# First expert product: 128 channels through the whole array, the last 64 for two chunks at a time in its two halves of rows

## Chip, cores and metric

One core of a Trainium2 chip. The metric is device time in microseconds (us). Medians are of four to seven runs. Block times, clock figures and profile lines are those of each kernel's one profiled run. Ratios are computed as the mean time of one kernel's runs over the mean of the other's from the same rounds, so they are not quite the ratios of the medians quoted beside them.

## The reference

A causal convolution over the sequence (7 taps, softmax weights a head) feeds a mixture of experts with 28,672 tokens, 192 channels (D), 8 experts and a hidden width of 1024 (F). A token goes to the expert with the largest logit, or, where its local gate is at least one half, to the one that the token before it went to. Its output is the softmax probability of that expert times two products:

```python
h = np.maximum(x[b, s] @ w1[e], 0.0)     # 192 -> 1024
out[b, s] = p[e] * (h @ w2[e])           # 1024 -> 192
```

All data are fp32.

## The kernel before

Three stages: convolve and route, place every token in a slot (all 256 slots of a block belong to one expert), then 119 expert blocks. Only the last stage changes much. Three block-long pieces of work go through PE (TensorE): the first product, four transposes for the next block, the second product. In short:

```python
DG = D + 1              # a token's row: its D values, then its gate
xp = pool(name="xp", bufs=4)        # gathered rows; wp, the weights, has 3 buffers

def load(i):            # weights of block i; its 256 rows by two indirect DMAs
    ...
    for k in range(2):
        nc.gpsimd.indirect_dma_start(out=xg[:, k, :], in_=rows[:, :], ...)   # L393

def turn(i, xg):        # rows -> channels on partitions, two halves of 96
    for d in range(2):
        for k in range(2):
            nc.tensor.transpose(xps[:, d, k*P:(k+1)*P], xg[:, k, d*DH:(d+1)*DH], identity=ident)
    nc.vector.tensor_copy(xT, xps)

def hidden(w1b, xT):    # first product, four PSUM banks of two chunks each
    for m in range(0, FK, 2):
        for u in range(2):
            for d in range(2):      # 96 + 96 channels
                nc.tensor.matmul(hps[:, u, :], lhsT=w1b[:, d, (m+u)*P:(m+u+1)*P],
                                 rhs=xT[:, d, :], start=(d == 0), stop=(d == 1))
        # eviction with relu: banks 0 and 2 on ScalarE (L419), 1 and 3 on VectorE (L417)

def output(i, w2b, xg, hT):
    ...                 # second product, 16 matmuls of 192 columns
    # scaling by the gate: first half on ScalarE (L434), second on VectorE (L432),
    # then two indirect DMAs scatter the rows

for i in range(NB):
    ...                 # load(i + 2)
    hT = hidden(w1b, xT)
    xT = turn(i + 1, ...)
    output(i, w2b, xg, hT)
```

The order in which each engine's instructions stand in the program is not the order of this text. A scheduler decides it from the dependencies and its own notion of time. It moves, for instance, the gather of a later block ahead as soon as one of the four `xg` buffers is free.

## Time and profile before

| | before |
|---|---|
| time, median | 2082.5 us |
| span of the profiled run | 2076.4 us |
| one expert block, from one scaling on ScalarE to the next | 12.55 us |
| first product, of that (32 records x 0.216) | 6.91 us |
| granted clock in the expert stage | full, no exception |

And a trap, in the page's list of DMAs (the last number is the median time from issue to landing):

```profile
xg<-rows,slot_tok POOLq DMA_INDIRECT x238, 9.1
```

These 9.1 us come from a handful of gathers at the start, behind the first weight loads. In steady blocks the trace's semaphore updates show the second gather landing 2.55 us after its issue.

### The profile page before, as it was taken

The page shows a single profiled execution, that of the slowest core. Times are in us where ns is not written, and L with a number is a line of the kernel's source. Part 1 is how long each engine was busy: PE and PEld are TensorE (multiplying, and loading weights), DVE is VectorE, ACT ScalarE, POOL GpSimd, SP SyncE. Part 2 cuts the span into 40 slices and gives each one's busy share as a digit, 9 for nine tenths or more (in the row PEclk, how much of TensorE's full clock was granted, in tenths as well). Part 3 has the DMA queues.
Part 4 walks back from the last instruction along what each step waited for, and adds up shares of the span by engine and source line. Part 5 has one row for each costly group of instructions (what it writes and reads, how often), then busy time and mean ns, then how long its engine had stood idle before and what let it go on. Part 6 is the DMA issues. An engine that isn't in the chain of part 4 may idle for free. (4 is left out here: it accounts for less than half of the span.)

```text
span 2076.4 us, 25966 instructions
## 1 busy us (share of the span) xinstructions
PE 1953.5 (94%) x10208; PEld 1679.0 (81%) x10208; DVE 594.2 (29%) x1648; ACT 257.6 (12%) x487; POOL 494.7 (24%) x521
## 2 busy tenths in 40 slices
PE   2989889589699999999999999999999999999998
PEld 1868667511199999999999999999999999999997
DVE  5333333599711111111111112111111211111111
ACT  0211112000011111111111111111111111111111
POOL 3000000000123333333333333333333333333331
PEclk9989879555599999999999999999999999999999
DMA  3362441300265555555555555555555555555551
GB/s 107 104 160 88 130 121 40 98 9 1 61 175 152 160 162 156 154 159 157 153 155 163 157 153 156 163 155 153 162 161 154 153 160 158 152 158 163 156 154 34
DMA packets 111547, 278.60 MB, mean 134 GB/s; under 512 B 12639, under 2 KB 77367, under 8 KB 100002
## 3 DMA queue, kind: packets, MB, share of 16 engines
q1 hardware_dynamic: 59536, 209.24, 34.3%
q0 software_dynamic: 22848, 45.58, 7.5%
q10 hardware_dynamic: 29042, 22.14, 4.4%
q8 instruction: 80, 1.31, 0.3%
q14 instruction: 41, 0.34, 0.0%
HBM read 232.74 MB, written 45.53 MB: 134 GB/s over the span
## 5 line engine op out<-in xcount | busy, mean ns | idle before, releaser
L414 PE MATMUL hps<-xT,w1b 96*128 96x256 f32 x3808 | 843.2, 379 | 0.0
L414 PEld LDWEIGHTS hps<-xT,w1b 96*128 96x128 f32 x3808 | 721.2, 190 | 93.3
L426 PE MATMUL yps<-w2b,hT 128*128 128x192 f32 x3808 | 638.5, 326 | 0.0
L426 PEld LDWEIGHTS yps<-w2b,hT 128*128 128x128 f32 x3808 | 616.1, 190 | 0.1
L437 POOL DMA_INDIRECT out_dram<-o_sb,slot_tok x238 | 240.6, 1011 | 963.4 <-ACT o_sb L434 859.1
L417 DVE TENSOR_SCALAR hT<-hps 128x512 f32<-128x512 f32 x238 | 164.5, 691 | 638.3 <-PE hps L414 638.3
L393 POOL DMA_INDIRECT xg<-rows,slot_tok x238 | 232.9, 979 | 230.2 <-DVE slot_tok L366 154.5
L419 ACT ACTIVATE hT<-hps 128x512 f32<-128x512 f32 x238 | 142.1, 597 | 675.8 <-PE hps L414 673.0
L432 DVE TENSOR_SCALAR o_sb<-yps,xg 128x192 f32<-128x192 f32 x119 | 49.7, 418 | 572.7 <-ACT o_sb L434 572.7
L434 ACT ACTIVATE o_sb<-yps,xg 128x192 f32<-128x192 f32 x119 | 50.0, 420 | 804.9 <-PE yps L426 784.5
L358 PE MATMUL sps<-at_hi,at_lo 128*128 128x476 bf16 x224 | 124.4, 555 | 24.5 <-DVE at_lo L352 13.0
L186 PEld LDWEIGHTS lps<-wg,yT 96*128 96x128 f32 x896 | 126.7, 215 | 16.5 <-ACT yT L183 8.0
L165 PE MATMUL cps<-x_sb,band 128*128 128x336 f32 x256 | 100.8, 478 | 31.2 <-DVE band L79 27.1
L186 PE MATMUL lps<-wg,yT 96*128 96x9 f32 x896 | 123.3, 265 | 3.8 <-DVE yT L181 3.4
L358 PEld LDWEIGHTS <-at_lo 128*128 128x128 bf16 x224 | 23.4, 105 | 124.7 <-DVE at_lo L352 124.7
L167 PE MATMUL cps<-x_sb,pband 128*128 128x336 f32 x256 | 98.2, 467 | 10.2 <-DVE pband L79 10.2
L165 PEld LDWEIGHTS cps<-x_sb,band 128*128 128x128 f32 x256 | 48.4, 201 | 52.6 <-DVE band L79 27.3
L402 PE MATMUL xps<-ident,xg 128*96 128x128 f32 x476 | 73.3, 275 | 13.6 <-DMA xg<-rows,slot_tok 13.6
L405 DVE COPY xT<-xps 96x512 f32<-96x512 f32 x119 | 80.5, 676 | 13.4 <-PE xps L402 13.4
L402 PEld LDWEIGHTS xps<-ident,xg 128*96 128x96 f32 x476 | 56.6, 127 | 29.3 <-issue 11.8
L167 PEld LDWEIGHTS cps<-x_sb,pband 128*128 128x128 f32 x256 | 49.4, 200 | 33.0 <-DVE pband L79 11.4
L177 PE MATMUL tps<-ident,y_sb 128*96 128x128 f32 x448 | 75.4, 295 | 0.0
(114 smaller groups left out, 532.4 us busy)
## 6 DMA issues: line engine op xcount, KB each, us to landing
w1b<-in_w_dram SPq DMA_DIRECT2D x119, 768.0 KB, 5.2
w2b<-in_w_dram SPq DMA_DIRECT2D x119, 768.0 KB
rows<-y_sb ACTq DMA_DIRECT2D x16, 1351.0 KB, 7.7
x_sb<-in_x_dram SPq DMA_DIRECT2D x16, 1344.0 KB, 6.5
xg<-rows,slot_tok POOLq DMA_INDIRECT x238, 9.1
out_dram<-o_sb,slot_tok POOLq DMA_INDIRECT x238, 2.4
w<-in_weight_dram SPq DMA_DIRECT2D x1, 28.0 KB
wg<-in_wgl_dram ACTq DMA_DIRECT2D x1, 6.8 KB
```

The costliest lines, as they stand in the source:

```text
L165: nc.tensor.matmul(cps, lhsT=band[:, h, :], rhs=x_sb[:, 1 + s:1 + s + CB, hc], start=True, stop=False)
L167: nc.tensor.matmul(cps, lhsT=pband[:, h, :], rhs=x_sb[:, s:s + CB, hc], start=False, stop=True)
L186: nc.tensor.matmul(lps[:, j + u, :], lhsT=yT[:, u, k, :], rhs=wg[:, k, :], start=(k == 0), stop=(k == 1))
L358: nc.tensor.matmul(sps, lhsT=at_lo, rhs=at_hi, start=(t == 0), stop=(t == T - 1))
L393: nc.gpsimd.indirect_dma_start(out=xg[:, k, :], out_offset=None, in_=rows[:, :], in_offset=bass.IndirectOffsetOnAxis(ap=slot_tok[:, n:n + ...
L402: nc.tensor.transpose(xps[:, d, k * P:(k + 1) * P], xg[:, k, d * DH:(d + 1) * DH], identity=ident)
L405: nc.vector.tensor_copy(xT, xps)
L414: nc.tensor.matmul(hps[:, u, :], lhsT=w1b[:, d, (m + u) * P:(m + u + 1) * P], rhs=xT[:, d, :], start=(d == 0), stop=(d == 1))
L417: nc.vector.tensor_scalar(hT[:, m:m + MH, :], hps, 0.0, None, Alu.max)
L419: nc.scalar.activation(hT[:, m:m + MH, :], hps, Act.Relu)
L426: nc.tensor.matmul(yps[:, k, :], lhsT=hT[:, m, k * P:(k + 1) * P], rhs=w2b[:, m, :], start=(m == 0), stop=(m == FK - 1))
L437: nc.gpsimd.indirect_dma_start(out=out, out_offset=bass.IndirectOffsetOnAxis(ap=slot_tok[:, n:n + 1], axis=0), in_=o_sb[:, k, :], in_offse ...
```

## The change

D is 192, so two passes of 96 rows leave a quarter of the array's rows idle. The change contracts 128 channels with the whole array (8 products) and the last 64 in one half of its rows each (8 products, alternating between the halves so that two can run at once). The halves need the 64 channels on partitions 0 to 63 and again on 64 to 127. So ScalarE copies them beside themselves in `xg` before the transposes. The core of the diff (gate moved to column 0 and weight layout cut):

```diff
-        xg = xp.tile([P, KT, DG], F32, name="xg")
+        xg = xp.tile([P, KT, DG + DR], F32, name="xg")          # DR = 64
...
     def turn(i, xg):
-        xps = xps_p.tile([DH, 2, BT], F32, name="xps")
+        nc.scalar.copy(xg[:, :, DG:], xg[:, :, 1 + P:DG])        # L400
+        xps = xps_p.tile([P, 2, BT], F32, name="xps")
...
     def hidden(w1b, xT):
+        hps = [hps_p.tile([P, 2, BT], F32, name="hps") for q in range(FK // 2)]
+        for s in range(FK):                                      # L415: 128 rows
+            nc.tensor.matmul(hps[s // 2][:, s % 2, :], lhsT=w1b[:, s * P:(s + 1) * P],
+                             rhs=xT[:, 0, :], start=(s % 2 == 0), stop=False, ...)
+        for half in range(2):
+            for j in range(2):
+                for row in range(2):                             # L424: 64 rows
+                    rows_ = slice(row * DR, (row + 1) * DR)
+                    c = F + (half * 2 + j) * P
+                    nc.tensor.matmul(hps[half * 2 + row][:, j, :], lhsT=w1b[rows_, c:c + P],
+                                     rhs=xT[rows_, 1, :], start=False, stop=True, ...)
+            # evictions: bank 2*half on ScalarE (L432), bank 2*half + 1 on VectorE (L430)
```

More of the change, by code (lines that the diff above doesn't have):

```diff
@@ L27 @@
 DH = D // 2
+DR = D - P
 FK = F // P
@@ L33 @@
 NS = NB * KT
-DG = D + 1
+DG = 1 + D
 SHIFT_P = P.bit_length() - 1
@@ L163, in conv @@
                 hc = slice(h * GS, (h + 1) * GS)
+                yc = slice(1 + h * GS, 1 + (h + 1) * GS)
                 cps = cps_p.tile([P, CB, GS], F32, name="cps")
@@ L169, in conv @@
                 if h % 2:
-                    nc.vector.tensor_copy(y_sb[:, s:s + CB, hc], cps)
+                    nc.vector.tensor_copy(y_sb[:, s:s + CB, yc], cps)
                 else:
-                    nc.scalar.copy(y_sb[:, s:s + CB, hc], cps)
+                    nc.scalar.copy(y_sb[:, s:s + CB, yc], cps)
         for j in range(0, NT, 2):
@@ L176, in conv @@
                 for k in range(2):
-                    nc.tensor.transpose(tps[:, u, k, :], y_sb[:, j + u, k * DH:(k + 1) * DH],
+                    nc.tensor.transpose(tps[:, u, k, :], y_sb[:, j + u, 1 + k * DH:1 + (k + 1) * DH],
                                         identity=ident)
@@ L250, in route @@
         nc.vector.tensor_reduce(pr, ex, axis=AX.X, op=Alu.add)
-        nc.vector.tensor_tensor(y_sb[:, :, D], pr, rs, op=Alu.mult)
+        nc.vector.tensor_tensor(y_sb[:, :, 0], pr, rs, op=Alu.mult)
         for s in range(0, NT, CB):
@@ L378, in experts @@
     yps_p = ctx.enter_context(tc.tile_pool(name="yps_p", bufs=2, space=PSUM))
-    MH = 512 // BT
     def load(i):
@@ L383, in load @@
                            skip_runtime_bounds_check_because="a count of at most 7")
-        w1b = wp.tile([DH, 2, F], F32, name="w1b")
-        nc.sync.dma_start(out=w1b.rearrange("p k f -> p (k f)"),
-                          in_=w1[bass.ds(e, 1)].rearrange("o p x -> (o p) x"))
+        w1b = wp.tile([P, F + F // 2], F32, name="w1b")
+        nc.sync.dma_start(out=w1b, in_=w1[bass.ds(e, 1)].rearrange("o p x -> (o p) x"))
         w2b = wp.tile([P, FK, D], F32, name="w2b")
@@ L393, in load @@
             nc.gpsimd.indirect_dma_start(
-                out=xg[:, k, :], out_offset=None, in_=rows[:, :],
+                out=xg[:, k, :DG], out_offset=None, in_=rows[:, :],
                 in_offset=bass.IndirectOffsetOnAxis(ap=slot_tok[:, n:n + 1], axis=0))
@@ L402, in turn @@
                 nc.tensor.transpose(xps[:, d, k * P:(k + 1) * P],
-                                    xg[:, k, d * DH:(d + 1) * DH], identity=ident)
-        xT = tp.tile([DH, 2, BT], F32, name="xT")
+                                    xg[:, k, 1 + d * P:1 + (d + 1) * P], identity=ident)
+        xT = tp.tile([P, 2, BT], F32, name="xT")
         nc.vector.tensor_copy(xT, xps)
@@ L409, in hidden @@
         hT = hp.tile([P, FK, BT], F32, name="hT")
-        for m in range(0, FK, MH):
-            hps = hps_p.tile([P, MH, BT], F32, name="hps")
-            for u in range(MH):
-                for d in range(2):
-                    nc.tensor.matmul(hps[:, u, :], lhsT=w1b[:, d, (m + u) * P:(m + u + 1) * P],
-                                     rhs=xT[:, d, :], start=(d == 0), stop=(d == 1))
-            if (m // MH) % 2:
-                nc.vector.tensor_scalar(hT[:, m:m + MH, :], hps, 0.0, None, Alu.max)
-            else:
-                nc.scalar.activation(hT[:, m:m + MH, :], hps, Act.Relu)
+        hps = [hps_p.tile([P, 2, BT], F32, name="hps") for q in range(FK // 2)]
+        for s in range(FK):
+            nc.tensor.matmul(hps[s // 2][:, s % 2, :], lhsT=w1b[:, s * P:(s + 1) * P],
+                             rhs=xT[:, 0, :], start=(s % 2 == 0), stop=False,
+                             skip_group_check=True)
+        for half in range(2):
[4 more added lines that the diff above has]
+                    nc.tensor.matmul(hps[half * 2 + row][:, j, :], lhsT=w1b[rows_, c:c + P],
+                                     rhs=xT[rows_, 1, :], start=False, stop=True,
+                                     skip_group_check=True)
+            for row in range(2):
+                q = half * 2 + row
+                if row:
+                    nc.vector.tensor_scalar(hT[:, 2 * q:2 * q + 2, :], hps[q], 0.0, None, Alu.max)
+                else:
+                    nc.scalar.activation(hT[:, 2 * q:2 * q + 2, :], hps[q], Act.Relu)
         return hT
@@ L429, in output @@
         for k in range(KT):
-            gate = xg[:, k, D:D + 1]
+            gate = xg[:, k, 0:1]
             if k % 2:
@@ L451, in experts, with _w1_layout @@
         output(i, w2b, xg, hT)
+def _w1_layout(np, w1):
+    rest = w1[:, P:, :].reshape(E, DR, 2, 2, 2, P)
+    rest = rest.transpose(0, 3, 1, 2, 4, 5).reshape(E, P, F // 2)
+    return np.concatenate([w1[:, :P, :], rest], 2)
 def kernel(**inputs):
@@ L466 @@
         .reshape(2, DH, E + 1).transpose(1, 0, 2).reshape(DH, 2 * (E + 1)),
-        "w1": i["moe_w1"].reshape(E, 2, DH, F).transpose(0, 2, 1, 3).reshape(E, DH, 2 * F),
+        "w1": _w1_layout(_np, i["moe_w1"]),
         "w2": i["moe_w2"].reshape(E, FK, P, D).transpose(0, 2, 1, 3).reshape(E, P, FK * D),
```

## The prediction

> **What bounds the kernel now.** I read the page first: busy shares, then the strip of 40 slices.
>
> ```profile
> PE 1953.5 (94%) x10208; PEld 1679.0 (81%) x10208; DVE 594.2 (29%) x1648; ACT 257.6 (12%) x487; POOL 494.7 (24%) x521
> ...
> PE   2989889589699999999999999999999999999998
> ...
> PEclk9989879555599999999999999999999999999999
> ...
> L414 PE MATMUL hps<-xT,w1b 96*128 96x256 f32 x3808 | 843.2, 379 | 0.0
> ...
> L426 PE MATMUL yps<-w2b,hT 128*128 128x192 f32 x3808 | 638.5, 326 | 0.0
> ```
>
> From slice 12 on (about 575 us, to 2070) the expert blocks run: PE at nine tenths in every slice, full clock, no idle time before either product. The first product (L414), which the change touches, is the dearest group, 843.2 us. 3808 records are 119 blocks x 32: 16 products a block, each two records because the data are fp32. The mean of 379 ns is latency; start to start in the trace's records two of them are 0.216 us apart, so 32 take 6.91 us.
>
> Then I read the timeline of one block, all engines. Columns: start, length, engine, line, operation, in brackets the idle time before it.
>
> ```profile
> 1000.22 7.07 PE L414 MATMUL hps<-xT,w1b 96*128 96x256 f32 x32
> ...
> 1000.42 0.42 ACT L434 ACTIVATE o_sb<-yps,xg 128x192 f32<-128x192 f32 x1 [6.77 <-PE yps L426]
> 1000.87 0.42 DVE L432 TENSOR_SCALAR o_sb<-yps,xg 128x192 f32<-128x192 f32 x1 [4.81 <-ACT o_sb L434]
> 1001.11 1.01 POOL L437 DMA_INDIRECT out_dram<-o_sb,slot_tok  x1 [7.25 <-ACT o_sb L434]
> 1002.19 0.60 ACT L419 ACTIVATE hT<-hps 128x512 f32<-128x512 f32 x1 [1.36 <-PE hps L414]
> 1002.42 0.99 POOL L393 DMA_INDIRECT xg<-rows,slot_tok  x1 [0.30 <-issue]
> 1003.72 0.97 POOL L393 DMA_INDIRECT xg<-rows,slot_tok  x1 [0.30 <-issue]
> ...
> 1007.12 0.60 PE L402 MATMUL xps<-ident,xg 128*96 128x128 f32 x4
> ...
> 1007.56 5.37 PE L426 MATMUL yps<-w2b,hT 128*128 128x192 f32 x32
> ...
> 1012.76 1.03 PE L414 MATMUL hps<-xT,w1b 96*128 96x256 f32 x4
> ...
> 1012.97 0.42 ACT L434 ACTIVATE o_sb<-yps,xg 128x192 f32<-128x192 f32 x1 [6.77 <-PE yps L426]
> ```
>
> PE runs first product, four transposes, second product with no gap; from one scaling by ScalarE (L434) to the next is 12.55 us (over 111 blocks: 12.549 to 12.552). So the matmul stream alone sets the period. ScalarE waits most of it. What matters later: right after block i is scaled (1000.42, 1000.87), GpSimd issues a scatter and then the two gathers of a **later** block, into the buffer that block i has just left (four buffers of xg).
>
> **What the Trainium skill says.** (1) "TensorE: Matmul & The Clock Gate", Part 3, The mechanism: matmuls in different row groups run at the same time, starting about 4 ns apart, and start and end in program order. No run here shows it yet; the kernel before has no such pair. (2) The same page, LDWEIGHTS: the time goes by columns, P/1.2 ns, so 107 ns for 128 columns whatever the rows. The trace agrees: the tiny gate products (9 moving columns, 128 stationary ones) follow each other every 0.112 us. Two loads in one 0.216 us slot are 0.224: just about hidden. (3) "TensorEngine Tiling (Array Packing)", Key Properties: changing the tiling mode drains TensorE. No duration is given and none is in this trace. (4) "TensorE: Matmul & The Clock Gate", Architectural detail: ScalarE and VectorE take their instructions strictly in order. This decides my number.
>
> **The change part by part.**
>
> *Products.* 16 products of 96 rows become 8 of 128 rows and 8 of 64 rows in the halves of the array. The 8 full ones are 16 records x 0.216 = 3.46 us. The 8 halves alternate rows 0 and 64 with each in its own PSUM bank. As each product is two records on the same half, in-order starting pairs the second of one with the first of the next: 16 records in about 9 slots, 9 x 0.216 = 1.94 us. Together 5.40 against 6.91: 1.51 us saved, less two drains (unknown, I allow 0.1). PE's own period becomes about 12.55 - 1.5 = 11.05 us, and 119 x 1.5 = 179 us would give some 1903 us. This is the intent.
>
> *Transposes.* Four still, of 128 columns for 96; 0.109 us apart before, little changed. VectorE's copy of them (676 ns for 512 columns) costs the same.
>
> *Weights.* 128 x 1536 x 4 bytes as before 96 x 2048 x 4: 786 KB. Moving the gate to column 0 costs nothing.
>
> *The added copy.* ScalarE copies the last 64 channels beside themselves, 128 elements a partition. Two ScalarE activations from SBUF to SBUF in this trace took 0.249 us for 56 and 0.390 for 224 columns, so about 0.31 us (estimate). Against ScalarE's 12% that is nothing. But **where** it stands is not: in the built order of the changed program ScalarE's sequence is: scale block i, copy for block i+4, evict hidden bank 0 of block i+1, evict bank 2. The copy waits for both gathers of block i+4. Those go into the buffer that block i is just leaving, so they can't be issued before the scaling that stands immediately ahead of the copy. So in every block ScalarE stops until a gather issued moments ago has landed, and only then evicts the hidden bank that the second product waits for.
>
> How long is that? Set t at the start of ScalarE's scaling. Gathers are issued at t+2.0 and t+3.3, the second is written out by t+4.3. The page gives 9.1 us to landing for them, but from only a few gathers at the start, while six weight loads were in the queue; I used the trace's semaphore updates of the landings in 111 steady blocks instead: last landing at t+5.86 median, 6.10 mean, 10% at 7.0 or later. Then 0.04 to the consumer (gathers at the start: landing 568.15, transposes 568.19), copy 0.31, eviction 0.60, 0.05 to PE (as in the convolution's yT), 0.15 for a weight load with nothing ahead of it. Second product starts at t + 6.10 + 0.04 + 0.31 + 0.60 + 0.05 + 0.15 = t+7.25. Before it started at t+7.146. It and what follows take 12.55 - 7.146 = 5.40. New period 7.25 + 5.40 = **12.65 us**, against 12.55.
>
> So the saving (PE would be ready at about t+5.7) turns into a PE wait of about 1.5 us in each block. Sum: 115 blocks with a gather in front, +0.10 each, +12 us; the last four have none and gain 1.5 each, -6. 2082.5 + 6 = 2088.
>
> **The rivals.**
>
> *A, the full gain:* ScalarE isn't held up, 1903 us. It speaks for it that PE is the bound and everything else has room. Against: the built order, and the gather issue at 1002.42 and 1003.72, after both scalings. For a full gain the gathers would have to land by about t+4.5; the earliest of 111 landed at 5.68. Even at that the period is 12.23, 38 us less: 2045.
>
> *B, no overlap of the halves:* drains, weight loads or PSUM keep them apart. Then the product stays near 6.9 us and PE is ready at t+7.15 as before; only late landings hurt. Taking for each block the later of the two, some 80% stay at 7.15 and the rest average about 8.3: period about 12.8, 2110 us. So even the mechanism of the change moves the total little.
>
> *C, gathers land later than before:* the first product ends 1.5 us sooner, so the next w1 load (1007.32 before) is issued at about t+5.2, near the landing, and takes DMA engines. Each 0.1 us of landing is 12 us of the total; 0.3 more gives 2125.
>
> *D, the clock drops in the new gap.* In the convolution, runs of 3.4 us stretches in which I reckon PE streamed for only 0.32 to 0.41 of the time kept the full clock, and it fell only around 0.2. A 1.5 us gap leaves over 0.5. Unlikely.
>
> **Range and chances.** The centre is 2088. The landing (6.10, plausibly 5.8 to 6.5 in the new rhythm) gives -35 to +46 us, the small latencies some 0.1 us a block, 12 us. Range 2050 to 2140. Faster by over 2% (under 2041) needs either rival A or landings all at the minimum: 0.07. Slower by over 2% (over 2124) needs C, or B with some of C: 0.14. Within: 0.79.
>
> **What would show it.** In the profile after: the records of the full and the half products together take about 5.4 us a block (a mean start-to-start of 0.108 for the halves; 0.216 would be B). A new ScalarE group, the copy, of about 0.3 us x 119, with idle time before it of some 5.3 us each released by the gather's DMA. Idle time of PE before the second product of about 1.5 us x 115, released by ScalarE's eviction. Period of the scalings near 12.65, the last four shorter. The clock at full. I am wrong if ScalarE's copy does not stand before the eviction when run, if landings move by more than 0.35 us, or if the gap costs clock.

## More of the kernel before

In the view of waits a line reads: who waited, on which line, for whom; total us; how often; the longest. Two lines of the kernel before:

```profile
ACT hT L419 <- PE hps L414: 673.0, 237, 181.8
...
PE xps L402 <- DMA xg<-rows,slot_tok: 13.6, 4, 10.6
```

ScalarE waits nearly always for PE, which costs nothing as long as PE is the bound. PE waited for gathered rows four times, all at the start of the stage: the gathers run far enough ahead that their landing never shows.

## The result and the profile after

| | before | after |
|---|---|---|
| time, median (lowest to highest) | 2082.5 (2080.9 to 2083.6) | 2104.1 (2103.0 to 2112.8) |
| ratio | | 1.0117 (95%: 1.0097 to 1.0137) |
| block, median | 12.55 us | 12.42 us |
| block, mean (111 steady blocks) | 12.55 us | 12.83 us |
| last blocks without a gather in front | | 11.17 us |
| expert stage, first to last scaling | 1480.3 us | 1514.9 us |
| clock at half in the expert stage | none | 13 stretches, 54.6 us |

The time lies inside the predicted range, 16 us above its centre, and within 2% of the kernel before. The profiled run of the changed kernel was the slowest of its four (2112.8 us, granted clock 0.920; the others had 0.924 to 0.927), so the clock figures here are those of a run 9 us above the median. The page of the changed kernel:

```profile
PE 1851.0 (88%) x10208; PEld 1516.2 (72%) x10208; DVE 595.3 (28%) x1648; ACT 269.3 (13%) x606; POOL 496.1 (24%) x521
...
PE   2989889589799999889899989999998999899987
...
PEclk9988879555599999989999999999999999999999
...
L439 PE MATMUL yps<-w2b,hT 128*128 128x192 f32 x3808 | 674.5, 337 | 142.7 <-ACT hT L432 142.7
...
L415 PE MATMUL hps<-xT,w1b 128*128 128x256 f32 x1904 | 432.0, 380 | 0.0
...
L424 PE MATMUL hps<-xT,w1b 64*128 64x256 f32 x1904 | 237.7, 389 | 0.0
...
L400 ACT COPY xg<-xg 128x128 f32<-128x128 f32 x119 | 35.8, 301 | 858.4 <-DMA xg<-rows,slot_tok 832.9
```

PE is no longer at nine tenths throughout, and its busy share fell from 94% to 88% although the time grew: it has less to do and waits. The wait has a name: 142.7 us before the second product, released by ScalarE's eviction. The two groups of the first product cost 432.0 + 237.7 = 669.7 us of busy time, against 843.2. The last line is the added copy: 0.30 us each, as estimated, but 858 us of idle time on ScalarE in front of it, nearly all ended by a gather's DMA (172 us of it is one wait before the stage begins, the rest about 5.8 us a block). The timeline of one block shows how that becomes PE's wait:

```profile
1013.84 3.62 PE L415 MATMUL hps<-xT,w1b 128*128 128x256 f32 x16
...
1014.04 0.42 ACT L447 ACTIVATE o_sb<-yps,xg 128x192 f32<-128x192 f32 x1 [5.07 <-PE yps L439]
...
1016.06 0.99 POOL L393 DMA_INDIRECT xg<-rows,slot_tok  x1 [0.30 <-issue]
1017.35 0.97 POOL L393 DMA_INDIRECT xg<-rows,slot_tok  x1 [0.30 <-issue]
...
1017.39 2.00 PE L424 MATMUL hps<-xT,w1b 64*128 64x256 f32 x16
...
1019.32 0.66 PE L404 MATMUL xps<-ident,xg 128*128 128x128 f32 x4
...
1020.08 0.30 ACT L400 COPY xg<-xg 128x128 f32<-128x128 f32 x1 [5.62 <-DMA xg<-rows,slot_tok]
1020.29 1.08 ACT L432 ACTIVATE hT<-hps 128x512 f32<-128x512 f32 x2
...
1020.93 5.47 PE L439 MATMUL yps<-w2b,hT 128*128 128x192 f32 x32 [0.95 <-ACT hT L432]
...
1026.44 0.42 ACT L447 ACTIVATE o_sb<-yps,xg 128x192 f32<-128x192 f32 x1 [5.07 <-PE yps L439]
```

Read it downwards. Block i is scaled (1014.04). Two gathers are issued for the block four ahead, into the buffer just left. Both products are done at about 1019.3 and PE transposes. ScalarE could have evicted bank 0 as soon as VectorE evicted bank 1 (1018.60, a line left out here). Instead it stands at the copy until the rows land (1020.08, after 5.62 us of idle time). Only then come the two evictions, and PE starts the second product at 1020.93 instead of about 1019.8. The period from scaling to scaling is 12.40 us here, and PE's own work in it is 11.17.

The mean is worse than the median. Of 111 steady blocks, 21 had a landing over 0.3 us later than the median (t+5.77, counted from the scaling). In 13 of them a 16 KB instruction packet was started on a DMA engine between t+3.2 and t+5.0; only two other steady blocks had such a packet. In six of the other eight the gather belongs to the last block of an expert, where many empty slots read one and the same row. The kernel before has its late landings at mostly the same blocks, hidden because the rows are needed more than two blocks later. And after 13 of the longer gaps the clock fell. One such product, after a gap of 2.22 us:

```profile
1341.13 7.15 PE L439 MATMUL yps<-w2b,hT 128*128 128x192 f32 x32 [2.22 <-ACT hT L432]
```

The same 32 records took 5.47 us above. The trace has the granted clock at half for 3.4 us from 1341.7 on.

### The profile page after: what moved, and what is told of

Its sections match the earlier page's. It is cut to its first block, busy times and chain, and to the rows that moved or that the text cites. A ratio compares the mean times of both kernels' runs of the same rounds, so it can differ in the third digit from the quotient of the medians.

```text
span 2111.1 us, 25970 instructions
## 1 busy us (share of the span) xinstructions
PE 1851.0 (88%) x10208; PEld 1516.2 (72%) x10208; DVE 595.3 (28%) x1648; ACT 269.3 (13%) x606; POOL 496.1 (24%) x521
## 5 line engine op out<-in xcount | busy, mean ns | idle before, releaser
L439 PE MATMUL yps<-w2b,hT 128*128 128x192 f32 x3808 | 674.5, 337 | 142.7 <-ACT hT L432 142.7
L439 PEld LDWEIGHTS yps<-w2b,hT 128*128 128x128 f32 x3808 | 639.6, 196 | 170.6 <-ACT hT L432 170.6
L415 PE MATMUL hps<-xT,w1b 128*128 128x256 f32 x1904 | 432.0, 380 | 0.0
L415 PEld LDWEIGHTS hps<-xT,w1b 128*128 128x128 f32 x1904 | 359.7, 191 | 43.5
L424 PE MATMUL hps<-xT,w1b 64*128 64x256 f32 x1904 | 237.7, 389 | 0.0
L424 PEld LDWEIGHTS hps<-xT,w1b 64*128 64x128 f32 x1904 | 174.1, 186 | 55.3 <-issue 39.5
L400 ACT COPY xg<-xg 128x128 f32<-128x128 f32 x119 | 35.8, 301 | 858.4 <-DMA xg<-rows,slot_tok 832.9
L432 ACT ACTIVATE hT<-hps 128x512 f32<-128x512 f32 x238 | 128.8, 590 | 13.7 <-PE hps L424 13.7
L404 PE MATMUL xps<-ident,xg 128*128 128x128 f32 x476 | 79.8, 290 | 10.5 <-DMA xg<-rows,slot_tok 10.5
L404 PEld LDWEIGHTS xps<-ident,xg 128*128 128x128 f32 x476 | 50.5, 142 | 51.4 <-DMA xg<-rows,slot_tok 29.1
```

Of the source, the lines that this page charges most:

```text
L404: nc.tensor.transpose(xps[:, d, k * P:(k + 1) * P], xg[:, k, 1 + d * P:1 + (d + 1) * P], identity=ident)
L415: nc.tensor.matmul(hps[s // 2][:, s % 2, :], lhsT=w1b[:, s * P:(s + 1) * P], rhs=xT[:, 0, :], start=(s % 2 == 0), stop=False, skip_group_c ...
L424: nc.tensor.matmul(hps[half * 2 + row][:, j, :], lhsT=w1b[rows_, c:c + P], rhs=xT[rows_, 1, :], start=False, stop=True, skip_group_check=True)
L432: nc.scalar.activation(hT[:, 2 * q:2 * q + 2, :], hps[q], Act.Relu)
L439: nc.tensor.matmul(yps[:, k, :], lhsT=hT[:, m, k * P:(k + 1) * P], rhs=w2b[:, m, :], start=(m == 0), stop=(m == FK - 1))
```

## The experiments

Unless the edit says otherwise, each is an edit of the changed kernel. All are correct against the reference.

| run | time, median us | ratio to before (95%) | block, median us | clock at half, us |
|---|---|---|---|---|
| changed kernel | 2104.1 | 1.0117 (1.0097 to 1.0137) | 12.42 | 54.6 |
| e1_pinned | 1920.7 | 0.9221 (0.9196 to 0.9246) | 11.17 | 0 |
| e2_bufs6 | 2112.9 | 1.0152 (1.0120 to 1.0184) | 12.44 | 41.0 |
| e3_copy_in_before | 2118.0 | 1.0145 (1.0104 to 1.0186) | 12.55 | 3.4 |
| e4_gpsimd_copy | 1914.4 | 0.9190 (0.9169 to 0.9211) | 11.17 | 0 |
| e5_unpaired | 2031.0 | 0.9741 (0.9704 to 0.9777) | 12.14 | 0 |
| e6_vector_copy | 2029.2 | 0.9739 (0.9711 to 0.9767) | 11.81 | 23.9 |
| e7_zero_rows | 2087.3 | 1.0021 (0.9992 to 1.0050) | 12.40 | 30.7 |
| e8_as_written | 1961.6 | 0.9417 (0.9396 to 0.9437) | 11.57 | 0 |
| e10_one_half | 2120.9 | 1.0187 (1.0164 to 1.0210) | 12.89 | 0 |
| e12_two_two | 1928.5 | 0.9260 (0.9239 to 0.9280) | 11.27 | 0 |

### e1_pinned: the same instructions, but the copy behind a scaling is for rows that landed long before

```diff
+    def double(xg):
+        tc.keep_in_program_order(nc.scalar.copy(xg[:, :, DG:], xg[:, :, 1 + P:DG]))
     def turn(i, xg):
-        nc.scalar.copy(xg[:, :, DG:], xg[:, :, 1 + P:DG])
...
+        if i + 1 < NB:
+            double(got[i + 1][2])
         hT = hidden(w1b, xT)
```

> Same instructions as the changed kernel, but ScalarE's copy is pinned one block before its use, for a block whose gathers landed long ago, so that it no longer waits for a gather just issued. Theory (the copy's place in ScalarE's order turned the gain into a wait): ScalarE's idle time before the copy on the gather's DMA vanishes, every block takes 11.17 us as the unstalled last blocks of the changed kernel did, 119 x (12.55 - 11.17) = 164 us under the kernel before: about 1918 us (1905 to 1935). Rival (the halves of the array, their drains or the clock eat the gain): stays above 2040 us.

Measured: 1920.7 us. Every block takes 11.17 us, the largest 11.174, although its gathers land as late as before (median t+5.79, one at t+10.67). One block:

```profile
1006.77 0.42 ACT L450 ACTIVATE o_sb<-yps,xg 128x192 f32<-128x192 f32 x1 [5.20 <-PE yps L442]
1007.09 0.29 ACT L400 COPY xg<-xg 128x128 f32<-128x128 f32 x1
...
1010.12 2.00 PE L427 MATMUL hps<-xT,w1b 64*128 64x256 f32 x16
...
1011.33 0.60 ACT L435 ACTIVATE hT<-hps 128x512 f32<-128x512 f32 x1 [3.95 <-issue]
...
1012.54 5.37 PE L442 MATMUL yps<-w2b,hT 128*128 128x192 f32 x32
...
1017.94 0.42 ACT L450 ACTIVATE o_sb<-yps,xg 128x192 f32<-128x192 f32 x1 [5.20 <-PE yps L442]
```

The copy (1007.09) now follows the scaling at once: it is for the block two ahead and not four ahead, and those rows landed long ago. The evictions start while the halves still run (1011.33), and PE goes from one product to the next without a gap. Nothing was taken from or added to any engine; ScalarE's copy costs 0.29 us and nobody waits for it. So the change's arithmetic is worth 8%, and the copy's place in ScalarE's order cost all of it.

### e2_bufs6: more row buffers

```diff
-    xp = ctx.enter_context(tc.tile_pool(name="xp", bufs=4))
+    xp = ctx.enter_context(tc.tile_pool(name="xp", bufs=6))
```

> The changed kernel with six row buffers instead of four. Theory (order): the gather now runs six blocks ahead, but the copy for it still stands right behind the scaling that frees its buffer, so ScalarE waits as before: within 1% of the changed kernel, 2090 to 2120 us, with some 800 us of ScalarE idle on the gather's DMA. Rival (too little prefetch: more buffers hide the landing): about 1918 us.

Measured: 2112.9 us, the changed kernel's time within the intervals. ScalarE's wait in the view of waits:

```profile
ACT xg L400 <- DMA xg<-rows,slot_tok: 825.9, 113, 171.9
```

Prefetching six blocks ahead changes nothing, because the copy is hoisted with the gather: it again stands right behind the scaling that frees its buffer. One detail moved, and it tells a cause. The late landings of the experts' last blocks came two blocks earlier, as the gathers did, while those beside instruction packets mostly stayed at the same blocks.

### e3_copy_in_before: the copy alone, in the kernel before

```diff
+        # in the gather of block i + 4, traced after the scaling of block i; result unused
+        tc.keep_in_program_order(nc.scalar.copy(xg[:, :, DG:], xg[:, :, P:D]))
...
-                nc.scalar.activation(hT[:, m:m + MH, :], hps, Act.Relu)
+                tc.keep_in_program_order(nc.scalar.activation(hT[:, m:m + MH, :], hps, Act.Relu))
```

(ScalarE's scaling is pinned in the same way, and the gathers are traced four blocks ahead, so that ScalarE's order is that of the changed kernel.)

> The kernel before (16 products of 96 rows) with the added copy alone, its result unused, in the same place of ScalarE's order as in the changed kernel. Theory (the wait alone sets the time): the second product starts at the later of t+7.15 and landing + 1.15, so most blocks keep 12.55 us and those with a late landing lose about 1 us: 2095 to 2125 us, close to the changed kernel though PE has 1.4 us more to do in each block. Rival (the wait is harmless and the new products are what costs): 2082 us within 6.

Measured: 2118.0 us.

```profile
ACT xg L399 <- DMA xg<-rows,slot_tok: 840.4, 116, 173.5
```

PE's products are those of before, yet the time is close to that of the changed kernel. Some 15 us of it are not the wait's: in this profiled run the expert stage began 15.6 us later than in the kernel before (first scaling at 602.0 us, not 586.4), and the edit changes nothing in the stages ahead of it. The stage itself took 1508.9 us, against 1480.3 before and 1514.9 in the changed kernel. Usual blocks keep 12.55 us, since PE takes that long anyhow; 19 with late landings take longer. So the wait by itself, with the old products, costs 28.6 us, and the new products behind it gain nothing in sum. That the two stages agree within 6 us is partly chance: usual blocks are 0.13 us longer here (12.55 against 12.42), but the clock fell only once, because PE's gaps are shorter.

### e5_unpaired, e10_one_half, e12_two_two: are the halves really simultaneous?

e5 and e12 keep e1's pinned copy; only the order of the half products differs (in e5 the evictions also stand behind all eight):

```diff
 # e5_unpaired: four upper products, then four lower
-        for half in range(2):
-            for j in range(2):
-                for row in range(2):
+        for row in range(2):
+            for half in range(2):
+                for j in range(2):
 # e12_two_two: two upper, two lower, two upper, two lower
-            for j in range(2):
-                for row in range(2):
+            for row in range(2):
+                for j in range(2):
```

> As the pinned version, but the eight half products are issued four on the upper rows, then four on the lower rows, so that none has a neighbour in the other half. Theory (the gain is the overlap of the two halves of rows): 16 records x 0.216 = 3.46 us instead of 1.93, +1.5 us in each block, 182 us over the pinned version: 2085 to 2115 us. Rival (half the rows cost half the time by themselves): equal to the pinned version, about 1918 us.

Measured: 2031.0 us, far under the expected 2085 to 2115, and far over the rival's 1918. The lines are the 16 half records and the transposes of a block:

```profile
1008.39 2.96 PE L427 MATMUL hps<-xT,w1b 64*128 64x256 f32 x16
1011.29 0.66 PE L407 MATMUL xps<-ident,xg 128*128 128x128 f32 x4
```

The halves took 2.90 us (1008.39 to 1011.29), where the changed kernel needs 1.93. The starts of the single records in the trace show why it is not 3.5: the upper half's eight start at 0, 0.32, 0.54, 0.75, 0.97, 1.18, 1.40 and 1.62 us, and a second series starts at 0.974, beside the fifth. My expectation had taken it that only neighbours in the program can overlap, and that failed. Two runs settle what happens. First, no overlap at all, all eight on the upper rows and no copy:

```diff
-                    rows_ = slice(row * DR, (row + 1) * DR)
+                    rows_ = slice(0, DR)
-        nc.scalar.copy(xg[:, :, DG:], xg[:, :, 1 + P:DG])
+        # w1b holds the last 64 channels' weights in rows 0 to 63, by a second DMA;
+        # the last two transposes have 64 columns
```

> After the unpaired order came out at 2031 us and not near 2100: all eight half products on the upper 64 rows, no copy, no ScalarE wait. Theory (only two different halves can overlap; the unpaired order still overlapped in its middle because the second half's records were taken ahead of the first's last ones): 16 records x 0.216 = 3.46 us for the halves, a block of about 12.7 us, 2090 to 2115 us in all. Rival (64 rows are faster than 128 by themselves): clearly under 2060 us.

Measured: 2120.9 us, just over the expected 2115, block 12.89 us:

```profile
1000.01 3.62 PE L418 MATMUL hps<-xT,w1b 128*128 128x256 f32 x16
1003.56 3.72 PE L427 MATMUL hps<-xT,w1b 64*128 64x256 f32 x16
1007.21 0.66 PE L406 MATMUL xps<-ident,xg 128*128 128x128 f32 x4
```

The halves take 3.65 us: one after another, 0.216 apart, each as dear as a product of 128 rows. Whole array and halves take 3.55 and 3.65 where 16 x 0.216 would be 3.46 each, so the two changes of mode (to half rows and back) cost 0.28 us together. The block is 12.89 - 12.55 = 0.34 us longer; the other 0.06 lies in the transposes, whose first two starts are 0.166 us apart and not 0.113 as before.

> As the pinned version, with the half products in the order upper, upper, lower, lower (four records of one half, then four of the other). In the unpaired order the lower half's first record started with the fifth of the upper's eight. Theory A (a half's records may start before up to three or four earlier, still waiting records of the other half): full overlap, 1920 us within 12, starts of upper and lower records 7 ns apart. Theory B (strictly in order, only neighbouring records overlap): three of eight slots more per group, about 11.17 + 6 x 0.216 = 12.4 us a block, some 2065 us.

Measured: 1928.5 us, as theory A said, with blocks of 11.27 us. The first upper and the first lower record start 13 ns apart. The lower one stands fifth in the program (the scheduler kept the half products of e5 and e12 in the order written), and records of one half never start closer than 0.216 us, as e10 shows. So it ran ahead of three upper records that had not yet started. In e5 the ninth record started beside the fifth: again ahead of three. So the order of the halves matters only beyond that reach; alternating, as in the change, is the best of the three by 0.10 and 0.97 us a block.

### e6_vector_copy, e4_gpsimd_copy, e8_as_written: other places for the copy

```diff
-        nc.scalar.copy(xg[:, :, DG:], xg[:, :, 1 + P:DG])
+        nc.vector.tensor_copy(xg[:, :, DG:], xg[:, :, 1 + P:DG])     # e6_vector_copy
+        nc.gpsimd.tensor_copy(xg[:, :, DG:], xg[:, :, 1 + P:DG])     # e4_gpsimd_copy
+        tc.keep_in_program_order(nc.scalar.copy(...same...))         # e8_as_written
```

> The changed kernel with the copy on VectorE, where it stands behind VectorE's scaling and before its eviction of bank 1. Theory (any engine that takes its instructions in order and owes PE an eviction hands on the wait): the second product starts on time, at about t+5.75, but its third chunk waits for bank 1, ready at landing + 0.9: some 0.4 us a block with usual landings, more with late ones: 1960 to 2030 us, between the pinned and the changed version. Rival (only ScalarE has this problem): 1920 us within 12.

Measured: 2029.2 us, as the theory said, at the upper end of its range.

```profile
1006.80 0.82 PE L439 MATMUL yps<-w2b,hT 128*128 128x192 f32 x4
...
1007.52 0.23 DVE L400 COPY xg<-xg 128x128 f32<-128x128 f32 x1 [5.62 <-DMA xg<-rows,slot_tok]
1007.66 1.28 DVE L430 TENSOR_SCALAR hT<-hps 128x512 f32<-128x512 f32 x2
...
1008.40 4.82 PE L439 MATMUL yps<-w2b,hT 128*128 128x192 f32 x28 [0.79 <-DVE hT L430]
```

Now VectorE stands at the copy until the landing (1007.52). PE starts the second product on time with the two chunks that ScalarE evicted, does four records, and waits for VectorE's bank until 1008.40. The wait is passed on by whichever in-order engine owes PE an eviction; it is smaller because PE needs VectorE's bank later.

> The changed kernel with the copy on GpSimd, which owes PE nothing. Theory (only an engine that stands between PE's two products hands on the wait): GpSimd waits for the landing itself, after its second scatter, and PE does not: 1920 us within 12, a block 11.17 us. Rival (GpSimd's wait delays the next scatters and gathers until they show): above 1950 us.

Measured: 1914.4 us, not told apart from e1 (the ranges of the runs overlap).

```profile
1004.39 5.37 PE L439 MATMUL yps<-w2b,hT 128*128 128x192 f32 x32
...
1005.93 0.29 POOL L400 COPY xg<-xg 128x128 f32<-128x128 f32 x1 [1.71 <-DMA xg<-rows,slot_tok]
```

GpSimd stands waiting too (1.71 us in front of the copy), but it owes PE nothing before the next block.

> The changed kernel with the copy pinned where it is written, behind both of ScalarE's evictions of the block before and ahead of the two transposes that read it. Theory: no wait for a gather any more, but PE's third transpose now waits for eviction (0.60) and copy (0.30) that start when the first product ends: about 0.8 us a block over the pinned version, some 95 us: 1995 to 2030 us, ScalarE's idle time on the gather's DMA gone. Rival (any place in order that does not wait for a gather is as good): 1920 us within 12.

Measured: 1961.6 us, better than the expected 1995 to 2030, worse than the rival.

```profile
1020.14 0.60 ACT L433 ACTIVATE hT<-hps 128x512 f32<-128x512 f32 x1 [0.22 <-issue]
...
1020.32 0.49 PE L440 MATMUL yps<-w2b,hT 128*128 128x192 f32 x2
1020.64 0.29 ACT L401 COPY xg<-xg 128x128 f32<-128x128 f32 x1
...
1020.98 0.44 PE L405 MATMUL xps<-ident,xg 128*128 128x128 f32 x2 [0.18 <-ACT hT L433]
```

The chain is as told: eviction (1020.14), copy (1020.64), transposes (1020.98). But the scheduler put two records of the second product between the first and the last two transposes, so a block loses 0.40 us (11.57 - 11.17) and not 0.8. The direction held; the size did not.

### e7_zero_rows: one cause of the late landings

```diff
-    rows = dram.tile([N + 1, DG], F32, name="rows")
+    rows = dram.tile([N + P, DG], F32, name="rows")      # a zero row for each partition
...
-    nc.vector.tensor_scalar(none, tok[:, 0, :], 0.0, float(N + P), Alu.is_equal, Alu.mult)
+    nc.vector.tensor_scalar(none, tok[:, 0, :], 0.0, pn, Alu.is_equal, Alu.mult)   # pn = N + P + p
```

> The changed kernel, but each of the 128 partitions has its own zero row for empty slots instead of one row for all. Theory (part of the late landings come from the last block of an expert, whose empty slots all read the same row, and the long gaps they cause cost clock too): in the changed kernel's profile the blocks concerned took about 33 us more than the usual 12.42, so 2065 to 2090 us, and fewer half-clock stretches in the expert stage than its 17. Rival (those late landings have another cause, such as instruction fetches): 2104 us within 8.

Measured: 2087.3 us, ratio 1.0021 against the changed kernel's 1.0117, and 8 half-clock stretches. (The "17" in the expectation was a miscount: the changed kernel has 13 stretches, 16 windows of 3.4 us.) The late blocks that vanished are those whose gather was for an expert's last block or for the empty blocks at the end; of the others most stayed. So the shared zero row was one cause. Of the 13 late blocks beside instruction packets ten stayed late; for those packets as their cause there is only the coincidence in time, in 13 of 21 blocks, which no run tested. Two blocks (the 27th and the 80th) stayed late as well; there GpSimd issued the second gather 1.8 us later than usual, and why is open.

## Why the prediction was right, step by step

**The products.** Right in sum. 5.40 us was predicted for whole and half products together; 5.48 was measured (1013.84 to 1019.32). The step inside it was not: I had the records shifted against each other in 9 slots, and they run in pairs 7 ns apart in 8, with about 0.2 us at the changes of mode making up the difference; that the sum came out was luck. PE's own period is 11.17 against 11.05.

**The wait.** Right, and e1, e2 and e3 show it as the cause: take the wait away and the gain is there, add it to the old products and the old kernel slows down. The chain from landing to the next scaling was predicted as 12.65 - 6.10 = 6.55 us and measured as 6.64 (median of 111 blocks). The landing was predicted unchanged at 6.10 in the mean and was 6.04. The single parts fit less well, and partly make up for each other: from the last recorded landing to the copy 0.27 us (0.04 predicted), from the copy's start to the eviction's 0.21 (0.31), from the second product to the next scaling 5.51 (5.40). The first is in part the trace's: it kept a median of 5 of a gather's 16 semaphore updates, and where it kept all 16 the copy started 0.10 us after the last. The wait of PE before the second product was about 1.0 us in usual blocks, less than the 1.5 predicted, as PE itself was ready later.

**Rival A** (full gain) lost to the built order, as argued. **Rival B** (no overlap) was not the case, but its claim that overlap hardly matters behind the wait was right: with the old products e3's expert stage took 28.6 us longer than the kernel before, and the rival had said 28 (2110 - 2082). **Rival C** (later landings through an earlier w1 load) did not show: 6.04 against 6.10, though with the lost updates allowed for (0.10 us ahead of the copy) the mean is nearer 6.2.

**Rival D, the clock, is the step that failed.** The prediction called it unlikely, from stretches of 3.4 us in the convolution with PE streaming for 0.32 to 0.41 of the time at full clock, and from the usual gap. The usual gap indeed cost no clock. But landings are not all usual: of the 21 late ones, 14 made a gap of 1.70 us or more before the second product, and after 13 of the 16 gaps of that size in the trace (two more are of blocks past the 111) the clock went to half for one or two windows of 3.4 us, 54.6 us in all.

Nor does the prediction's limit for a fall, "only around 0.2", come out of the traces. The changes of the clock lie on a grid of 3.41 us. As an estimate, let a record stream for its columns x 0.216/256 us. Then the kernel before lost the clock after windows with PE streaming for 0.30 to 0.34 of the time (windows of 0.38 and more kept it), and the changed kernel's expert stage after eight windows of 0.03 to 0.38 and five of 0.47 to 0.54. Four windows of 0.41 to 0.49 kept it there, and all from 0.58 up. So how a gap falls on the grid matters too.

Taking for each steady block the time above landing + 6.64, the trace has 18.9 us of extra time in 11 such blocks; in e3, which has the late landings but shorter gaps, the same sum is 1.5 us. The profiled run's expert stage was 34.6 us longer than before, where 6 were predicted; 18.9 of the missing 28.6 are this, and 7.7 are two blocks near the end (below). The median run, 16 us above the centre, lost less; it was not profiled. The sum should have had the tail of the landings go through the clock and not only through the wait.

**The last four blocks** were to gain 1.5 each without a gather in front. The last ones did (11.17), but the three blocks just before them, waiting for gathers of wholly empty blocks, took 14.6, 16.2 and 16.9.

## What to carry to other kernels

When a change adds a cheap instruction to an engine with room to spare, look in the built order at what stands in front of it and behind it: if it waits for a transfer issued moments before, everything behind it on that engine waits too, and more buffers do not help, since the scheduler hoists the copy with the transfer. Pin it next to work that is already late enough, or give it to an engine that owes the bound engine nothing; here that turned 1.012 into 0.92. And a mean landing time is not enough to size such a wait: the late ones also cost PE's clock.

## What the Trainium skill lacked or had wrong

- "TensorE: Matmul & The Clock Gate", Part 3, The mechanism, says that matmuls start and end strictly in program order. Starts do not when the row groups differ: in e12 a record of the lower half started 13 ns after the first of the upper half, ahead of three upper records that stood before it; in e5 likewise ahead of three. What ends first was not tested, as the ends are modelled. The page's 4 ns between partners were 7 ns here.
- "TensorEngine Tiling (Array Packing)", Key Properties, names the drain at a change of mode but gives no duration. Two changes a block, to half rows and back, cost 0.28 us in e10 (3.55 and 3.65 us for 16 records each, against 16 x 0.216).
- "TensorE: Matmul & The Clock Gate", Part 1, speaks of idle windows of about 3.4 us before the clock falls, and gives the rule of no PE gaps over about 3.4 us. Here gaps of PE of 1.70 to 2.22 us were often enough (8 of the 10 such gaps in the profile of the changed kernel, 3 of the 8 of 1.79 to 2.28 us in e2); gaps up to 1.66 us did not do it in either. The low stretches were 3.4 or 6.8 us long, which agrees with the page's window.
- No page that I read tells what many gathers of one row cost: giving the empty slots a row for each partition took the time from 1.0117 to 1.0021 of before (e7).
